# Logits, gate and row store of a chunk issued one loop step later in a gated linear attention + routed MoE kernel

## Chip, cores and metric

The kernel runs on one core of one Trainium2 chip. The metric is the device time of one execution in microseconds (us), the median of several runs. A core has five engines, each with its own instruction queue, worked off in order: TensorE (PE in the profile; its weight loads are PEld), VectorE (DVE), ScalarE (ACT), GpSimd (POOL) and SyncE (SP, which here only issues DMAs). The engines meet through semaphores: an instruction at the head of a queue that has to wait holds everything behind it on that engine.

## What is computed

A gated recurrence over 768 positions for 4 batches and 8 heads of width 48, whose output rows (3072 of 384 numbers) go through a mixture of 8 experts, each row through the expert with the highest logit:

```python
for t in range(S):
    state = alpha[:, :, t, :, None] * state + np.einsum('bhd,bhe->bhde', k[:, :, t], v[:, :, t])
    y[:, :, t] = np.einsum('bhd,bhde->bhe', q[:, :, t], state)
...
logits = x @ w_gate
expert_idx = np.argmax(logits, axis=1)
logits_s = logits - logits.max(-1, keepdims=True)
probs = np.exp(logits_s)
probs /= probs.sum(-1, keepdims=True) + 1e-09
gate_w = probs[np.arange(N), expert_idx]
...
    h = np.maximum(x_sorted[lo:hi] @ w1[e], 0.0)
    y_sorted[lo:hi] = h @ w2[e]
...
return (gate_w[:, None] * y).astype(np.float32)
```

Since the experts are piecewise linear without bias, a row can be scaled by its gate weight before it goes in.

## The kernel before

**Two halves.** The first (up to about 160 us) does the recurrence in 24 chunks of 128 positions (6 stretches of time for 4 batches; chunk s is batch s % 4 of stretch s // 4) and stores for each chunk 128 finished rows, scaled by their gate weight, to the scratch tensor x_rows. Then comes routing (lines 500 to 622) and the experts, which gather their rows from x_rows. Only the loop of the first half (lines 456 to 492) is touched by the change.

**The loop.** Its body is an order written out by hand under a manual schedule: each engine gets its instructions in the order of the calls, and step i mixes work on several chunks. `do(f, n)` calls f for chunk n if there is such a chunk. In step i, by engine:

- SP: `loads_for(i + 3)` starts the loads of a, v, k, q some chunks ahead, two chunks in each load, so a batch of four loads every other step; `keep_rows` issues the store of 128 rows (L411); `fetch_part` (L185, L188) one piece of the first expert's weights in steps 4 to 13; a small load at L264 once per four steps.
- PE: `scores(i)` (L311, into PSUM tiles sA and sB), at steps 4, 8, ... 20 `decay_cols` (L281, tile ep), `transposes(i + 1)` (L299, tile tp), `cums` (L250, tile cum, for chunk i + 5, the last in step 18), `read_state(i)` (L338), `attend(i)` (L348), `keys_values(i)` (L359), `rows(i - 1)` (L384: turned result back to rows, and the logits in the same product, into PSUM tile x).
- ACT: `result(i - 1)` (L367, copy of y to yT), `logs` (L244), the copy of the turned keys kT (L304), `cums`' two exponentials (L253, L254) and the issue of up to two tiny DMAs (L262: the one from icp for chunks 4 to 23, the one from cp for chunks 0 to 19), then `gate(i - 1)` (L402, an exponential and the reading of its accumulator) and `keep_rows(i - 1)` (L410, tile xs).
- DVE: `add_state(i - 1)` (L375/L377, tile acc), at a decay step the copy of E (L283), the two masked copies dA and dB (L319), the copy of the turned queries qT (L302), `decay_rows` (L269, L270) in the step ahead of a decay step, `logits(i - 1)` (L395, L396), two small operations of `gate` (L403, L404).
- POOL: `operands(i + 2)` (L289, two products), `scale_state(i)` (L326, tile U), and small things.

**What ties steps together.** Tiles sA, sB, x and cum have one buffer each (cum and ep share it), y is one tile for all steps. So `rows(i - 1)` may write x only after L395 and L410 have read the chunk before; `read_state(i)` may write y only after L367 and L377 have read chunk i - 1. yT and acc read different columns of y.

```python
            d["x"] = ps.tile([C, NP, C], F32, name="x")
...
            nc.vector.reduce_sum(lgn[:, t, :], d["x"][:, :, D2 : D2 + E].rearrange("p m e -> p e m"), axis=AX)
            nc.vector.tensor_reduce(lmin[:, t : t + 1], lgn[:, t, :], axis=AX, op=ALU.min)
...
            nc.scalar.activation(xs[:], d["x"][:, :, :D2], AF.Copy, scale=d["gw"][:])
            nc.sync.dma_start(x_d[t * C : (t + 1) * C, :], xs[:].rearrange("p m d -> p (m d)"))
```

Of the kernel before, what the change touches and what calls it, by code (L numbers as in the profile page):

```python
# [18 lines left out]
def kernel(  # L19
# [31 lines left out]
    NT = N // C  # L51
# [39 lines left out]
    def second_consts():  # L91
        nc.vector.tensor_scalar_mul(iw[:, :, D2:], iw[:, :, D2:], -1.0)
        for i in range(2):
            nc.vector.tensor_copy(
                iw[i * DP : (i + 1) * DP, :, i * D : (i + 1) * D],
                ident[i * DP : (i + 1) * DP, None, i * DP : i * DP + D].to_broadcast([DP, NP, D]),
            )
# [21 lines left out]
    def late_consts(i):  # L119
        if i == 0:  # L120
            nc.gpsimd.memset(lt_strict[:], 1.0)
            nc.gpsimd.affine_select(
                lt_strict[:], lt_strict[:], compare_op=ALU.is_gt, fill=0.0,
                base=0, pattern=[[1, C]], channel_multiplier=-1,
            )
            nc.gpsimd.memset(ones_sq[:], 1.0)
        if i == 1:
            nc.gpsimd.memset(zero_e[:], 0.0)
            nc.gpsimd.memset(keep[:], 1.0)
            nc.gpsimd.memset(keep[:, :, 0:1], 0.0)  # L130
        if i in (2, 3):
            for ti, tf, pattern, base, mult in list(iotas.values())[3 * (i - 2) : 3 * (i - 1)]:
                nc.gpsimd.iota(ti[:], pattern=pattern, base=base, channel_multiplier=mult)
                nc.gpsimd.tensor_copy(tf[:], ti[:])
            if i == 2:

                nc.gpsimd.memset(key0[:, 0:1], float(16 * N))
        if i == 4:

            nc.gpsimd.tensor_copy(iota_r[:], iota_f[:])  # L140
            nc.gpsimd.tensor_scalar(
                tok_n[:], tokv[:, NT // 2 :], scalar1=-1.0, scalar2=float(N // 2), op0=ALU.mult, op1=ALU.add,
            )
            nc.gpsimd.tensor_copy(tokv[:, NT // 2 :], tok_n[:])
# [33 lines left out]
    def fetch_part(g, i):  # L178

        if i == 0:  # L180
            g["w1"] = wpool.tile([C, DB, F], F32, name="w1")
            g["w2"] = wpool.tile([C, FB, Dm], F32, name="w2")
        if i < 6:
            a, h = i // 2, i % 2
            nc.sync.dma_start(g["w1"][:, a, h * F // 2 : (h + 1) * F // 2], moe_w1[0, a * C : (a + 1) * C, h * F // 2 : (h + 1) * F // 2])  # L185
        else:
            f = 2 * (i - 6)
            nc.sync.dma_start(  # L188
                g["w2"][:, f : f + 2], moe_w2[0, f * C : (f + 2) * C, :].rearrange("(a p) d -> p a d", p=C),
            )  # L190
# [27 lines left out]
    with tc.tile_pool(name="ld", bufs=6) as ld, \  # L218
# [23 lines left out]
        def logs(s):  # L242
            t = work.tile([C, Dm], F32, name="lna", bufs=4)
            nc.scalar.activation(t[:], st[s]["a"].rearrange("s h d -> s (h d)"), AF.Ln)  # L244
            st[s]["lna"] = t

        def cums(s):
            c, b = cb(s)
            cum = ps.tile([C, 512], F32, name="cum")
            nc.tensor.matmul(cum[:, :Dm], lhsT=cum_m[:], rhs=st[s]["lna"][:], start=True, stop=True)  # L250
            cp = work.tile([C, Dm], F32, name="cp", bufs=6)
            icp = work.tile([C, Dm], F32, name="icp", bufs=6)
            nc.scalar.activation(icp[:], cum[:, :Dm], AF.Exp, scale=-1.0)  # L253
            nc.scalar.activation(cp[:], cum[:, :Dm], AF.Exp)  # L254
            st[s]["cp"], st[s]["icp"] = cp, icp


            for cc, i, row in ((c, 1, icp[0:1, :]), (c + 1, 0, cp[C - 1 :, :])):
                if 0 < cc < NB:
                    if cc not in decay:  # L260
                        decay[cc] = work.tile([B, 2, Dm], F32, name="dec", bufs=3)
                    nc.scalar.dma_start(decay[cc][b : b + 1, i, :], row)  # L262
            if b == 0 and c + 1 < NB:
                nc.sync.dma_start(alpha0[:, c + 1], alpha[:, :, (c + 1) * C, :])  # L264

        def decay_rows(c):
            t = by_half(er[:B])
            d = decay[c].rearrange("b i (a p d) -> b i a p d", a=2, p=NP)
            nc.vector.tensor_tensor(t, d[:, 0], d[:, 1], op=ALU.mult)  # L269
            nc.vector.tensor_tensor(t, t, alpha0[:, c].rearrange("b (a p) d -> b a p d", a=2), op=ALU.mult)  # L270
# [7 lines left out]
        def decay_cols(c):  # L278
            ep = ps.tile([C, NP, C], F32, name="ep", tag="cum")
            for p in range(NP):  # L280
                nc.tensor.transpose(ep[:, p, :], pair(er[:], p), ident[:])  # L281
            decay[c] = work.tile([C, NP, B], F32, name="E", bufs=2)
            nc.vector.tensor_copy(decay[c][:], ep[:, :, :B])  # L283
# [130 lines left out]
        def do(f, i, *a):  # L414
            if 0 <= i < NT:
                f(i, *a)
# [4 lines left out]
        def sums_to(i):  # L421
            return {-2: 0, -1: 1, 0: 3, 1: 5}.get(i, -1 if i < 0 else min(i + 5, NT - 1))

        def new_sums(i):
            return range(sums_to(i - 1) + 1, sums_to(i) + 1)
# [10 lines left out]
        def loads_for(i):  # L436
            loads(("a", sums_to(i + 1)), ("v", i), ("k", i + 2), ("q", i + 2))

        def idle(n):

            t = ps.tile([C, NP, C], F32, name="sA")
            for _ in range(n):
                nc.tensor.matmul(t[:, :2, :], lhsT=er[:, 0].rearrange("s a d -> s (a d)"), rhs=er[:, :2], start=True, stop=True)
# [9 lines left out]
        nc.vector.memset(y[:], 0.0)  # L453
        first_consts()
        idle(4)
        for i in range(-4, NT + 1):
            loads_for(i + 3)
            do(scores, i)
            do(result, i - 1)
            do(add_state, i - 1)  # L460
            for s in new_sums(i + 1):
                logs(s)
            if 0 < i < NT and i % B == 0:
                decay_cols(i // B)
            do(mask, i, 0)
            do(mask, i, 1)
            if -2 < i < 0:
                idle(3)
            do(transposes, i + 1)
            sums = list(new_sums(i))  # L470
            for s in sums[:1]:
                cums(s)
            do(operands, i + 2)
            do(scale_state, i)
            if 0 < i + 1 < NT and (i + 1) % B == 0:
                decay_rows((i + 1) // B)
            do(read_state, i)
            do(attend, i)
            for s in sums[1:]:
                cums(s)  # L480
            do(keys_values, i)
            do(rows, i - 1)
            do(logits, i - 1)
            do(gate, i - 1)
            do(keep_rows, i - 1)
            if i == -3:
                second_consts()
            late_consts(i - 1)
            if 4 <= i < 14:
                fetch_part(groups[0], i - 4)  # L490
            if 15 <= i < 23:
                next(first_sums)
# [446 lines left out]
```

## Time and profile before

| what | value |
|---|---|
| median of 3 runs | 466.21 us (466.08 to 467.35) |
| the profiled execution, its own time | 467.84 us |
| its span | 466.0 us |
| granted TensorE clock, mean | 0.953 |
| busy: PE, DVE, ACT, POOL | 410.4, 229.8, 167.7, 140.2 us |
| copy of y to yT (L367), start for chunk 0, 3, 4, 14, 18, 19, 20, 23 | 17.72, 38.50, 45.01, 104.81, 128.87, 134.70, 140.87, 157.23 us |
| from one such start to the next, ordinary step | 5.82 to 5.84 us |
| the same, decay step 8, 12, 16 | 6.58 to 6.59 us |
| last logits (L395) | 159.56 us |

"Span" runs from the first to the last instruction that the profiler recorded; the execution's own time holds start and end besides. A line of the timeline gives start, duration, engine, line, operation, result and operands, and in brackets how long the engine had stood idle before it and what ended that. A PE line with x16 stands for sixteen matmuls one after the other. The start of the copy to yT comes once in each step, so its distances are the lengths of the steps.

### The profile page before, as it was taken

What the parts mean: (1) busy time and instruction counts of PE and PEld (TensorE: products, weight loads), DVE (VectorE), ACT (ScalarE), POOL (GpSimd) and SP (SyncE); (2) the same over time, 40 slices, a digit from 0 to 9 for tenths busy, and PEclk for the clock granted to TensorE, in tenths of its full rate; (3) what the DMA queues carried; (4) which work ended last, traced back from release to release, by engine and by line L of the source; (5) the groups of instructions that cost most, each with busy time, mean ns of one, the idle gap of its engine ahead of it and who ended that gap; (6) DMA issues with size and microseconds to landing.
All of it is one profiled execution on the core that took longest, in us unless ns stands there. A gap on an engine that the chain in (4) does not pass through costs nothing.

```text
span 466.0 us, 9245 instructions
## 1 busy us (share of the span) xinstructions
PE 410.4 (88%) x3548; PEld 350.4 (75%) x3548; DVE 229.8 (49%) x640; ACT 167.7 (36%) x454; POOL 140.2 (30%) x169
## 2 busy tenths in 40 slices
PE   7879999999987413799999999999999999999991
PEld 5657777777776401696996997997988988979970
DVE  3345454545455294357258258257356474473500
ACT  4564545454534200240351351440441522513511
POOL 3445444445663026500032032041140140200102
PEclk9999999999999555899999999999999999999997
DMA  9999999997621145303414415414423442400001
GB/s 178 213 181 214 216 201 216 211 240 167 137 70 35 40 146 193 109 0 136 152 41 188 153 38 188 153 48 175 153 88 133 169 170 64 152 1 18 30 1 49
DMA packets 119969, 59.07 MB, mean 127 GB/s; under 512 B 102806, under 2 KB 114159, under 8 KB 119924
## 3 DMA queue, kind: packets, MB, share of 16 engines
q1 hardware_dynamic: 114804, 48.80, 40.0%
q0 software_dynamic: 3424, 9.59, 5.9%
q8 instruction: 29, 0.48, 0.4%
q10 hardware_dynamic: 1696, 0.08, 0.2%
q14 instruction: 16, 0.13, 0.1%
HBM read 48.95 MB, written 9.58 MB: 126 GB/s over the span
## 4 chain that ended last, share of the span: by engine, by line
PE 57%; issue 7%; DVE 5%; ACT 3%; POOL 2%; DMA 1%; POOLq 0%; ACTq 0%; DVEq 0%
PE pA L729 12%; PE pB L729 9%; PE pA L785 8%; PE pC L800 8%; PE pC L729 5%; PE pB L785 4%; PE pC L785 2%; PE y L348 2%; PE x L384 2%; PE tp L647 2%; PE tp L830 1%; PE y L338 1%; ACT xs L410 1%; ACT yT L367 1%; PE sA L311 1%
## 5 line engine op out<-in xcount | busy, mean ns | idle before, releaser
L817 POOL DMA_INDIRECT out_dram<-zo,s_idx x29 | 31.8, 1096 | 210.0 <-ACT zo L816 114.3
L673 ACT COPY u<-pA 128x212 f32<-128x212 f32 (+7 forms) x80 | 25.5, 319 | 83.1 <-PE pA L785 77.6
L173 DVE TENSOR_TENSOR h_sb<-pB,u 128x212 f32<-128x212 f32 (+7 forms) x64 | 23.1, 362 | 64.0 <-PE pB L729 47.7
L800 PE MATMUL pC<-h_sb,w 128*128 128x424 f32 (+7 forms) x128 | 43.9, 496 | 0.0
L289 POOL TENSOR_TENSOR kqb<-k_sb,icp 128x384 f32<-128x384 f32 x24 | 25.5, 1062 | 60.6 <-PE y L359 23.2
L800 PEld LDWEIGHTS pC<-h_sb,w 128*128 128x128 f32 x128 | 24.1, 190 | 16.0 <-issue 6.7
L729 PE MATMUL pA<-t,s 128*128 128x212 f32 (+7 forms) x128 | 32.9, 339 | 2.4 <-issue 0.9
L637 POOL DMA_INDIRECT xg<-x_rows,g_idx x29 | 29.9, 1033 | 10.7 <-issue 6.4
L729 PE MATMUL pA<-xgT,w 128*128 128x212 f32 (+7 forms) x128 | 32.4, 335 | 0.0
L673 ACT COPY p<-pA 128x212 f32<-128x212 f32 (+7 forms) x40 | 13.1, 328 | 42.3 <-DVE t L176 26.9
L176 DVE TENSOR_TENSOR th<-h_sb,th 128x212 f32<-128x212 f32 (+7 forms) x64 | 23.2, 363 | 10.3 <-ACT h_sb L742 9.5
L311 PE MATMUL sA<-qT,kT 48*128 48x128 f32 x192 | 27.7, 284 | 0.2 <-DVE qT L302 0.2
L311 PE MATMUL sB<-qT,kT 48*128 48x128 f32 x192 | 27.7, 285 | 0.0
L402 ACT ACTIVATE gex<-lgn,lmin 128x8 f32<-128x8 f32 x24 | 7.2, 301 | 56.7 <-DVE lmin L396 54.5
L299 PE MATMUL tp<-ident,kqb 128*128 128x128 f32 x192 | 26.4, 279 | 1.2 <-POOL kqb L289 1.2
L729 PE MATMUL pC<-xgT,w 128*128 128x212 f32 (+7 forms) x128 | 27.4, 338 | 0.0
L729 PE MATMUL pB<-t,w 128*128 128x212 f32 (+7 forms) x128 | 27.0, 333 | 0.0
L311 PEld LDWEIGHTS sA<-qT,kT 48*128 48x128 f32 x192 | 23.1, 187 | 3.8 <-ACT kT L304 0.8
L384 PE MATMUL x<-iw,yT 128*64 128x104 f32 x384 | 23.0, 265 | 2.9 <-ACT yT L367 2.9
L742 ACT ACTIVATE h_sb<-h_sb 128x424 f32<-128x424 f32 (+7 forms) x32 | 17.1, 533 | 23.2 <-DVE h_sb L173 23.2
L785 PE MATMUL pA<-th,s 128*128 128x212 f32 (+7 forms) x128 | 24.6, 335 | 0.5 <-ACT u L673 0.5
L729 PEld LDWEIGHTS pA<-t,s 128*128 128x128 f32 x128 | 21.2, 190 | 4.9 <-ACT u L673 3.4
(176 smaller groups left out, 933.7 us busy)
## 6 DMA issues: line engine op xcount, KB each, us to landing
w<-in_moe_w_dram SPq DMA_DIRECT2D x14, 1536.0 KB, 7.4
x_rows<-xs SPq DMA_DIRECT2D x24, 192.0 KB, 2.1
a_sb<-in_alpha_dram SPq DMA_DIRECT2D x11, 384.0 KB, 4.3
k_sb<-in_k_dram SPq DMA_DIRECT2D x11, 384.0 KB, 5.7
q_sb<-in_q_dram SPq DMA_DIRECT2D x11, 384.0 KB, 5.3
v_sb<-in_v_dram SPq DMA_DIRECT2D x11, 384.0 KB, 5.6
w<-in_moe_w_dram SPq DMA_DIRECT2D x6, 256.0 KB, 3.7
w<-in_moe_w_dram SPq DMA_DIRECT2D x4, 384.0 KB, 3.8
```

The lines of the kernel that those rows point to most:

```text
L173: eng.tensor_tensor(out, a, b, op=ALU.add)
L176: eng.tensor_tensor(out, a, b, op=ALU.subtract)
L289: nc.gpsimd.tensor_tensor(by_half(kq[:, i]), d[n].rearrange("s (a p) d -> s a p d", a=2), d[e][:].rearrange("s (a p d) -> s a p d", a=2, p ...
L299: nc.tensor.transpose(tp[:, p, :], pair(kqb[s % 3][:, i], p), ident[:])
L311: nc.tensor.matmul(t[:, p, :], lhsT=d["kT"][r : r + D, p, :], rhs=d["qT"][r : r + D, p, :], start=True, stop=True,)
L384: nc.tensor.matmul(d["x"][o : o + HC, m, : D2 + E], lhsT=d["yT"][:, m // 2, m % 2, o : o + HC], rhs=iw[:, m, :], start=True, stop=True,)
L637: nc.gpsimd.indirect_dma_start(out=g["xg"][:r, j, :], out_offset=None, in_=x_d[:, :], in_offset=bass.IndirectOffsetOnAxis(ap=g["gi"](j, r) ...
L673: nc.scalar.copy(t[:, :m], bank["A"][:, :m])
L729: nc.tensor.matmul(out, lhsT=ops[n_][0], rhs=ops[n_][1], start=first and n_ == names[0], stop=True, skip_group_check=True,)
L785: nc.tensor.matmul(out, lhsT=lhs, rhs=rhs, start=first and f == 0, stop=True, skip_group_check=True)
L800: nc.tensor.matmul(d2[:, :n], lhsT=w2[:, f, 2 * C :], rhs=h[:, f, :n], start=(f == 0), stop=(f == FB - 1),)
L817: ins = nc.gpsimd.indirect_dma_start(out=out[:, :], out_offset=bass.IndirectOffsetOnAxis(ap=g["si"](j, r), axis=0), in_=zo[:r], in_offset= ...
```

## The change

In step i, `logits`, `gate` and `keep_rows` now work on chunk i - 2 in place of i - 1. `logits` stands behind the masks and ahead of `transposes`, `gate` and `keep_rows` stand behind `transposes` and ahead of `cums`. `rows` keeps its place at the end of the step. The loop has one step more, in which only these three have a chunk. Nothing is added or removed otherwise: the same instructions with the same shapes.

```diff
-        for i in range(-4, NT + 1):
+        for i in range(-4, NT + 2):
...
             do(mask, i, 1)
             if -2 < i < 0:
                 idle(3)
+            do(logits, i - 2)
             do(transposes, i + 1)
+            do(gate, i - 2)
+            do(keep_rows, i - 2)
             sums = list(new_sums(i))
...
             do(keys_values, i)
             do(rows, i - 1)
-            do(logits, i - 1)
-            do(gate, i - 1)
-            do(keep_rows, i - 1)
             if i == -3:
                 second_consts()
```

On each engine the order of a step becomes: DVE acc, (E), dA, dB, lgn, lmin, qT, the two of gate, (decay rows); ACT yT, lna, kT, gex, xs, icp, cp, the DMA issues of L262; SP the loads, then the store of chunk i - 2, then the small load and the weight piece; PE and POOL as before.

## Prediction
> **What bounds the kernel now.** I read the table by stages first. TensorE is near full in the chunk loop, and the clock is granted in full until the loop's end:
>
> ```profile
> 60.00:80.00 20.00, 19.10 (x307) 15.32 (x304) 9.57 (x30) 9.85 (x26) 9.28 (x11) 1.00 1.01 212
> 135.00:152.00 17.00, 13.21 (x225) 11.20 (x226) 9.00 (x25) 6.09 (x16) 7.54 (x9) 1.00 0.11 38
> 152.00:165.00 13.00, 5.64 (x67) 4.74 (x56) 4.57 (x22) 2.42 (x7) 0.00 (x0) 0.54 0.12 44
> ```
>
> The columns are PE, PEld, DVE, ACT, POOL, then the clock. 19.10 of 20 says that little can be won in the steady loop, but a modelled busy time can hide short waits. So I read the timeline of one ordinary step:
>
> ```profile
> 74.42 0.58 ACT L410 ACTIVATE xs<-x,gw 128x384 f32<-128x384 f32 x1 [0.47 <-PE sB L311]
> 74.90 0.58 ACT L367 COPY yT<-y 128x512 f32<-128x512 f32 x1
> 75.58 0.36 DVE L377 TENSOR_TENSOR acc<-y,U 128x192 f32<-128x192 f32 x1 [1.24 <-ACT yT L367]
> 75.85 0.68 DVE L319 TENSOR_TENSOR dA<-sA,cmask 128x512 f32<-128x512 f32 x1
> 76.08 0.66 PE L338 MATMUL y<-qT,U 48*48 48x128 f32 x16 [0.23 <-DVE acc L377]
> 76.25 0.51 ACT L253 ACTIVATE icp<-cum 128x384 f32<-128x384 f32 x1
> 76.80 0.51 ACTq L262 DMA_DIRECT2D dec<-icp  x1
> 77.40 0.54 ACTq L262 DMA_DIRECT2D dec<-cp  x1
> 78.02 0.90 PE L384 MATMUL x<-iw,yT 128*64 128x104 f32 x16
> 78.97 0.19 DVE L395 TENSOR_REDUCE lgn<-x 128x8 f32<-128x32 f32 x1 [1.24 <-PE x L384]
> 79.19 0.16 DVE L396 TENSOR_REDUCE lmin<-lgn 128x1 f32<-128x8 f32 x1
> 79.39 0.30 ACT L402 ACTIVATE gex<-lgn,lmin 128x8 f32<-128x8 f32 x1 [2.24 <-DVE lmin L396]
> 79.81 0.15 DVE L403 TENSOR_SCALAR gw<-gw 128x1 f32<-128x1 f32 x1 [0.46 <-ACT gex L402]
> 80.00 0.16 DVE L404 RECIPROCAL gw<-gw 128x1 f32<-128x1 f32 x1
> 80.26 0.58 ACT L410 ACTIVATE xs<-x,gw 128x384 f32<-128x384 f32 x1 [0.48 <-DVE gw L404]
> ```
>
> It is a ring. From x, lgn, lmin, gex and gw lead to xs; behind xs on ACT stands yT; acc waits for yT; read_state (L338) waits for acc, and leads through attend to the next rows (L384). ACT is idle 2.24 + 0.48 us in it, although y was ready for yT long before. Length 5.83 us.
>
> **The new order, step by step.** Let 0 be the start of scores.
>
> *PE without waits* (starts to starts, cum from 21.19 to 22.03, the last five from 40.45 to 43.13): scores 1.09, transposes 0.93, cum 0.84, read_state 0.58, attend 0.47 + 0.44, keys 0.36, rows 0.83: 5.54. A decay step has ep besides, 0.49: 6.03. So the most to win is 0.29 in an ordinary step and 6.59 − 6.03 = 0.56 in a decay step (0.48 in step 4).
>
> *A new ring, on ACT and DVE.* xs now stands behind kT and ahead of icp, cp and the two DMA issues; behind those stands the next step's yT. On DVE acc stands ahead of the masks, and the masks, lmin and qT ahead of gw. The hops: xs to icp 0.48 (as xs to yT); icp to the end of the second issue 1.69 (76.25 to 77.94); to yT 0.08; yT to acc 0.68; acc to dA 0.27; dA, dB 0.60 each; lgn to lmin 0.22; lmin to qT 0.08 (an operation that waits for nothing starts some 0.08 ahead of the end of the one before); qT 0.60; gw to reciprocal 0.19; to xs 0.26. Sum 5.75. gex hides beside qT: gw needs lmin + 0.62, qT gives lmin + 0.68. Does a DMA issue hold ACT back? Two rows say so:
>
> ```profile
> 17.12 0.50 ACTq L262 DMA_DIRECT2D dec<-cp  x1
> 17.72 0.59 ACT L367 COPY yT<-y 128x512 f32<-128x512 f32 x1 [0.63 <-ACT cp L254]
> ...
> 30.14 1.20 ACTq L262 DMA_DIRECT2D dec<-cp  x1
> 31.39 0.30 ACT L402 ACTIVATE gex<-lgn,lmin 128x8 f32<-128x8 f32 x1 [1.51 <-DVE lmin L396]
> ```
>
> yT and gex start 0.10 and 0.05 behind the issue; lmin had ended at 30.57. Today the issues lie in the 2.24 us in which ACT idles; that cover goes. The Trainium skill (DMA: Bandwidth & Descriptors, Issuing engines are not separate DMA queues) calls the sequencer time of an issue usually small beside its DMA; here 1.05 us per step stands on the path. Left at nothing, the rule makes the steady loop TensorE-bound (459.9 below).
>
> *Who waits behind it.* rows(i−1) is the added wait: x has one buffer, so it waits for xs(i−2). In the ring xs starts at 4.29, ends 4.87, rows can start at 4.92 where PE is there at 4.71: 0.21 idle per step, with the next scores queued behind. A decay step: ep ends at 1.75, E at 1.80, dA 1.88, xs 4.43, rows 5.06, before PE's 5.20: TensorE-bound at 6.03. POOL is covered: U ends 2.57 behind keys (78.20 to 80.77), read_state comes 3.69 behind. kT, qT end well ahead of the next scores.
>
> *SP.* The store waited for xs until 1.99 behind the next scores; now xs ends 0.9 ahead of them, so the loads behind it come 2.9 earlier. What covers them now: k and q of chunk 14 issue at 72.71 and 75.24, land after 5.7 and 5.3 (medians), and are used at 84.17 and 85.42, some 5 us later.
>
> *Steps 15 to 18* have one issue (1.05 in place of 1.69): ring 5.11, so PE's 5.54 and 6.03 hold. Step 15 still begins behind two: 5.75.
>
> *Steps without cum* (19 on): scores end at 1.16, dA 1.21, xs 3.76 (dA to xs 2.55), ends 4.34, rows 4.39, next scores 5.22, PE waiting for xs. Before: step 19 5.82, steps 21 and 22 5.06 and 5.05. Here the change loses 0.16 and 0.17, for gw now stands behind masks and qT. Step 20 (decay): rows 5.06, 5.89 against 6.02.
>
> *End.* Step 23 has no qT: xs 3.70, rows 4.33 against 4.44. rows(23) no longer waits for xs(22) and then yT(23), only for xs(22): 157.38 against 157.86.
>
> *Start.* Step 1 loses its gate: yT(1) can start at 23.87 in place of 25.21. But the second cum of step 2 waits for exponentials that now stand behind xs(0): about 28.75 against 28.00. With the later steps followed through, scores(4) start between 36.4 and 37.0, against 36.62. I take 0, bounds −0.4 and +0.3.
>
> **Sum of gains.** Ordinary steps 5 to 14: 8 × 0.08 = 0.64. Decay steps 4, 8, 12: 0.48 + 0.56 + 0.56 = 1.60. Steps 15 to 18: 0.08 + 0.55 + 0.29 + 0.29 = 1.21. Step 19: 0.60. Steps 20 to 22: 0.13 − 0.33 = −0.20. End: 0.11 + 0.48 = 0.59. Together 4.44. The profiled execution took 467.84 (span 466.0), 1.63 above the median of 466.21; routing and experts should not change, so 467.84 − 4.44 = 463.40, and against the median **461.8 us**.
>
> **The clock** could spoil the end. It was granted in full to about 152 and at 0.54 from then, behind a wait of PE of 1.58 us ahead of 151.70. In the new steps 21 and 22 PE waits about 0.9 once per step, where it waited 0.56. From no row can I read how much idling is allowed; if the clock fell one step earlier, step 22's 4.34 us of matmuls would double: bounds 0 and 4.3; I take 0, 0.9 being nearer to 0.56 than to 1.58. The Trainium skill (TensorE: Matmul & The Clock Gate, Part 1) has the clock halve after about 3.4 us of idleness in a window; by it the sum stays as it is.
>
> **Rivals.**
> 1. *The issues hold nothing* (both rows above being chance): xs to yT is 0.48 + 0.39 + 0.46 in place of 2.25, the ring 4.83, and PE bounds all steps to 18. Nine steps gain 0.21 more: 1.9, **459.9**. Against it: those two rows.
> 2. *The loads set the pace to step 14.* The DMA share is 1.01 in 60 to 80 us. Then 4 to 14 gain nothing (−2.24): **464.0**. Against it: SP stands idle 54.83 to 56.79 and 66.44 to 69.20, waiting for xs, and slack of 5 us.
> 3. *Slower: long DMA issues, now on the path.* The second issue took 1.20 at 30.14 and 1.67 at 41.73 (0.55 median), both hidden today. At 1.20 throughout, the ring is 6.40: the eight ordinary steps and step 15 lose 0.57 in place of gaining 0.08 (−5.85), decay steps take 6.48 in place of 6.03 (−1.35): **469.0**. From a mean of 0.63 an ordinary step is longer than before, from about 0.96 the whole kernel (9 × 0.41 + 3 × 0.23 is 4.4; a decay step's copy of E gives it 0.18 of slack). For it: loads now start nearer to these issues. Against it: 18 of 20 were short, beside running loads too.
> 4. *It moves the wait and wins nothing in the end*: PE waits for xs where it waited for acc, the waits of 0.9 are what the clock's governor counts, and the clock falls a step sooner: 461.8 + 4.3 = **466.1**. For it: the clock fell in this same stretch, behind waits of 0.56 and 1.58. Against it: 0.56 per step did not do it for steps 21 and 22.
>
> **Chances.** Forecast 0.52, rival 1 0.14, rival 2 0.12, rival 3 0.13, rival 4 0.09. The likeliest alone lies between 460.6 and 463.2 (ring ± 0.1 over eight steps, start ± 0.4). For eight in ten: down to 459.6, up to 465.6. About 0.3%, 1.4 us, can be told from no change. Faster 0.76 (the first three cases, nearly whole), same 0.11, slower 0.13.
>
> **What would show it.** yT starting 0.1 behind the second L262; acc, dA following at 0.68 and 0.95; rows waiting some 0.2 for xs in ordinary steps to 14 and 0.9 in 19, 21, 22; steps of 5.75, 6.03, then 5.54; L395's last near 155. I am wrong if ordinary steps stay at 5.83 or more, if read_state or the operands wait for a load, or if the clock falls before 147.

## The result, and the profile after

The changed kernel takes 461.22 us (median of 4 runs, 460.72 to 464.09) where the kernel before took 466.78 beside it (4 runs, 466.08 to 468.21): a ratio of 0.989, with a 95% interval of 0.984 to 0.994. The profiled execution took 461.57 us, its span is 459.7 (before: 467.84 and 466.0), at a mean granted clock of 0.956 (0.953).

The timeline of one ordinary step after the change, with ACT, DVE and, from PE, the product rows:

```profile
73.20 0.59 ACT L367 COPY yT<-y 128x512 f32<-128x512 f32 x1 [0.84 <-PE x L384]
...
73.89 0.36 DVE L377 TENSOR_TENSOR acc<-y,U 128x192 f32<-128x192 f32 x1 [2.90 <-ACT yT L367]
74.16 0.68 DVE L319 TENSOR_TENSOR dA<-sA,cmask 128x512 f32<-128x512 f32 x1
...
75.36 0.18 DVE L395 TENSOR_REDUCE lgn<-x 128x8 f32<-128x32 f32 x1
...
75.65 0.68 DVE L302 COPY qT<-tp 128x512 f32<-128x512 f32 x1
...
76.43 0.16 DVE L404 RECIPROCAL gw<-gw 128x1 f32<-128x1 f32 x1
76.62 0.58 ACT L410 ACTIVATE xs<-x,gw 128x384 f32<-128x384 f32 x1 [0.46 <-DVE gw L404]
...
77.26 0.93 PE L384 MATMUL x<-iw,yT 128*64 128x104 f32 x16
77.61 0.50 ACTq L262 DMA_DIRECT2D dec<-icp  x1
78.21 0.55 ACTq L262 DMA_DIRECT2D dec<-cp  x1
78.80 0.58 ACT L367 COPY yT<-y 128x512 f32<-128x512 f32 x1 [0.84 <-PE x L384]
```

The rows give 5.60 us from yT to yT, and every hop can be read as a distance of starts. yT begins at 78.80, where the second issue ends at 78.76; the release that the bracket names, rows, is not what came last. DVE works from acc to the reciprocal without a gap, then ACT from xs through icp, cp and the two issues to yT: the two halves of the new ring. The old one is gone: gex no longer stands on ACT waiting for the logits of rows that PE has only just finished.

The lengths of the steps, from the start of scores in one step to the next, tell where the time went (both profiled executions):

| steps | before | after |
|---|---|---|
| start of scores(4) | 36.62 | 36.73 |
| 4, 8, 12, 16 (decay) | 6.51, 6.58, 6.57, 6.58 | 5.88, 5.88, 6.39, 5.89 |
| 5, 6, 7 | 5.82, 5.83, 5.83 | 5.65, 5.60, **6.58** |
| 9, 10, 11 | 5.83, 5.83, 5.84 | **6.20**, 5.60, 5.60 |
| 13, 14, 15 | 5.84, 5.83, 5.83 | 5.68, 5.61, 5.60 |
| 17, 18 | 5.83, 5.83 | 5.44, 5.45 |
| 19, 20 | 5.82, 6.02 | 5.16, 5.84 |
| 21, 22 | 5.06, 5.05 | 5.22, 5.23 |
| start of scores(23) | 148.95 | 145.23 |

Three steps are out of line: 7, 9 and 12. ACT's timeline tells of 7 and 12:

```profile
58.94 0.58 ACT L410 ACTIVATE xs<-x,gw 128x384 f32<-128x384 f32 x1 [1.44 <-DMA x_rows<-xs]
...
83.82 1.24 ACTq L262 DMA_DIRECT2D dec<-cp  x1
85.10 0.59 ACT L367 COPY yT<-y 128x512 f32<-128x512 f32 x1 [1.54 <-issue]
```

In step 7, xs waits for a store of x_rows to land, because tile xs has two buffers and the store of two chunks ago still reads one. In step 12 a single issue takes 1.24 us and yT stands behind it; so it is in step 9, with one of 1.19 at 66.37.

The stages of the changed kernel in the windows (PE, PEld, DVE, ACT, POOL, clock, DMA share, GB/s):

```profile
60.00:80.00 20.00, 19.45 (x309) 16.05 (x306) 8.83 (x28) 11.26 (x28) 8.93 (x11) 1.00 1.04 223
...
148.00:152.70 4.70, 1.35 (x24) 0.89 (x20) 1.00 (x7) 2.42 (x7) 0.00 (x0) 1.00 0.12 44
152.70:165.00 12.30, 2.65 (x20) 2.26 (x20) 8.84 (x42) 0.97 (x3) 0.00 (x0) 0.50 0.12 35
```

PE is still not full between 60 and 80 us, 19.45 of 20. At the end the clock is whole until 152.70, and half from there. Before, it was already halved when rows(22) began. The last two products rows (of chunks 22 and 23) of the changed kernel, from PE's timeline:

```profile
149.69 0.93 PE L384 MATMUL x<-iw,yT 128*64 128x104 f32 x16 [1.27 <-ACT xs L410]
152.73 1.65 PE L384 MATMUL x<-iw,yT 128*64 128x104 f32 x16 [2.11 <-ACT xs L410]
```

Only rows(23) is slow here (1.65), where before rows(22) at 153.39 took 1.61 and rows(23) 1.65. The last logits (L395) start at 154.43 in place of 159.56.

### The profile page after: what moved, and what is told of

Read it like the earlier page. It is cut to its first block, busy times and chain, and to the rows that moved or that the text cites. A ratio compares the mean times of both kernels' runs of the same rounds, so it can differ in the third digit from the quotient of the medians.

```text
span 459.7 us, 9241 instructions
## 1 busy us (share of the span) xinstructions
PE 410.2 (89%) x3548; PEld 351.1 (76%) x3548; DVE 228.4 (50%) x640; ACT 171.1 (37%) x454; POOL 140.5 (31%) x169
## 4 chain that ended last, share of the span: by engine, by line
PE 64%; DVE 10%; issue 8%; DMA 6%; ACT 5%; POOL 2%; SPq 2%; ACTq 1%; POOLq 0%; DVEq 0%
PE pA L729 12%; PE pB L729 9%; PE pA L785 8%; PE pC L800 8%; PE pC L729 5%; PE pB L785 4%; PE x L384 3%; PE sA L311 3%; PE pC L785 2%; DMA w<-in_moe_w_dram 2%; DVE dA L319 2%; DVE dB L319 2%; DVE qT L302 2%; PE tp L647 2%; PE y L348 2%
## 5 line engine op out<-in xcount | busy, mean ns | idle before, releaser
L729 PE MATMUL pA<-t,s 128*128 128x212 f32 (+7 forms) x128 | 33.2, 341 | 1.0 <-ACT u L673 0.4
L729 PE MATMUL pA<-xgT,w 128*128 128x212 f32 (+7 forms) x128 | 32.4, 335 | 0.0
L729 PE MATMUL pC<-xgT,w 128*128 128x212 f32 (+7 forms) x128 | 27.4, 338 | 0.0
L729 PE MATMUL pB<-t,w 128*128 128x212 f32 (+7 forms) x128 | 27.0, 333 | 0.0
L384 PEld LDWEIGHTS x<-iw,yT 128*64 128x64 f32 x384 | 18.2, 140 | 9.9 <-ACT xs L410 9.4
L289 POOL TENSOR_TENSOR kqb<-q_sb,cp 128x384 f32<-128x384 f32 x24 | 24.7, 1029 | 2.1 <-DMA q_sb<-in_q_dram 2.1
L377 DVE TENSOR_TENSOR acc<-y,U 128x192 f32<-128x192 f32 x16 | 5.7, 358 | 39.0 <-ACT yT L367 26.7
```

What stands on the lines that cost most here:

```text
L289: nc.gpsimd.tensor_tensor(by_half(kq[:, i]), d[n].rearrange("s (a p) d -> s a p d", a=2), d[e][:].rearrange("s (a p d) -> s a p d", a=2, p ...
L384: nc.tensor.matmul(d["x"][o : o + HC, m, : D2 + E], lhsT=d["yT"][:, m // 2, m % 2, o : o + HC], rhs=iw[:, m, :], start=True, stop=True,)
L729: nc.tensor.matmul(out, lhsT=ops[n_][0], rhs=ops[n_][1], start=first and n_ == names[0], stop=True, skip_group_check=True,)
```

## Experiments

The theory: in the changed kernel a ring over ACT and DVE sets an ordinary step, and the two DMA issues of L262 are a part of it; before, they lay in ACT's idle time. The rivals: the issues hold nothing; TensorE or the loads set the step; the moved logits and gate gain by themselves. Where a line number in these profiles is larger by one or two, the edit has added lines above.

### The issues doubled, after and before

Each DMA of L262 is issued a second time from ACT, into a scratch tensor that nothing reads.

```diff
+        spare = nc.dram_tensor("spare", (NT, 2, Dm), F32, kind="Internal").ap()
...
                     nc.scalar.dma_start(decay[cc][b : b + 1, i, :], row)
+                    nc.scalar.dma_start(spare[s : s + 1, i, :], row)
```

In the changed kernel:

> The changed kernel, with each of the small DMAs of L262 issued a second time from ACT, into a scratch tensor that nobody reads. Ring theory (an issue holds ACT, and it now stands between xs and the next yT): each step up to 14 gets about 1.15 us longer (two more issues of 0.55 to 0.60), ordinary steps 5.60 -> 6.75, steps 15 to 18 about 5.6; whole kernel 471 to 475 us. Rival (issues hold nothing, TensorE is the bound): steps stay at 5.60, whole kernel 461 us, within 1.

Measured 474.70 us (2 runs), 1.016 of the kernel before (1.012 to 1.020), and 13.5 above the changed kernel. Its timeline on ACT:

```profile
79.39 0.44 ACTq L264 DMA_DIRECT2D spare<-icp  x1
...
80.49 0.45 ACTq L264 DMA_DIRECT2D spare<-cp  x1
80.98 0.59 ACT L369 COPY yT<-y 128x512 f32<-128x512 f32 x1 [1.78 <-PE sB L313]
```

Two more issues of 0.44 and 0.45 make an ordinary step 6.55 in place of 5.60, and yT again stands right behind the last of them. Steps 17 and 18 issue one DMA of L262, now two; they stay at 5.45 and 5.44. There xs to yT takes 2.02, which makes the ring 5.44, no longer than PE's own work in a step. So where the ring is the longest path, the issues are on it at their full price.

In the kernel before:

> The kernel before with the same doubling. Ring theory: ACT idles 2.24 us behind these issues until lmin comes, so 1.15 us more are hidden: ordinary steps stay at 5.83, whole kernel 466 to 468 us (the first steps with two prefix sums may lose 1 us). Rival (an issue costs the same wherever it stands): 11 steps of +1.15, 478 us or more.

Measured 470.01 us (8 runs), ratio 1.006 (1.004 to 1.009). Two places of ACT's timeline:

```profile
25.25 0.30 ACT L404 ACTIVATE gex<-lgn,lmin 128x8 f32<-128x8 f32 x1 [1.77 <-DMA spare<-icp]
...
80.80 0.45 ACTq L264 DMA_DIRECT2D spare<-cp  x1
81.74 0.30 ACT L404 ACTIVATE gex<-lgn,lmin 128x8 f32<-128x8 f32 x1 [2.24 <-DVE lmin L398]
```

In the steady loop the last of four issues ends at 81.25, and gex begins 0.5 later, when lmin is ready: hidden, and most ordinary steps stay at 5.83. The loss is larger than expected and comes for the most part from the start (scores(4) at 38.57 in place of 36.62), where steps 1 and 2 each have two cumulated sums and so eight issues. Step 2 takes 9.67 in place of 6.81. The gex at 25.25 (before: 23.86) stands behind issues that end at 25.21, though lmin had ended at 23.55; so xs comes 1.61 later in the step. For the rest of the step's loss, the granted clock fell: 0.69 between 28 and 33 us, where it was 1.00, and rows took 1.62 in place of 0.90.

### The issues on SP instead of ACT, after and before

```diff
-                    nc.scalar.dma_start(decay[cc][b : b + 1, i, :], row)
+                    nc.sync.dma_start(decay[cc][b : b + 1, i, :], row)
```

In the changed kernel:

> The changed kernel with the small DMAs of L262 issued from SP in place of ACT. Ring theory: xs to yT falls from 2.18 to about 1.35, the ring to 4.8, TensorE bounds the ordinary steps at about 5.44 (as in step 17 today), and the two long issues (1.19 and 1.24 us) cost nothing any more: 8 x 0.16 + 1.3 = 2.6 us less than the changed kernel, 458 to 459 us. Rival (ring broken but the loads behind the new waits on SP come late): operands wait for k or q, 461 us or more.

Measured 481.01 us (4 runs), ratio 1.029 (1.026 to 1.033): a miss. Steps 5, 6 and 9 do come at 5.44 or 5.45, so with the issues gone from ACT the ring is gone too. But SP works its queue off in order, and the small transfers now stand behind the bulk loads. Once issued they land after 1.9 and 2.2 us (medians; from ACT in the changed kernel 3.8 and 3.5), so it is their turn in the queue that comes late. The waits of this kernel (total, times, longest), from 41 to 130 us:

```profile
DVE er L269 <- DMA dec<-icp: 26.2, 4, 7.9
```

Step 4 takes 14.73. Neither the theory's 458 to 459 us nor the rival's late k and q foresaw this. The edit is not clean: it removes one cost and adds another.

In the kernel before:

> The kernel before with the small DMAs issued from SP. Ring theory: they lay in 2.24 us of idle ACT time, so nothing changes: ordinary steps 5.83, 466 to 467 us. Rival (ACT was short of time in the kernel before as well): faster by 2 us or more.

Measured 483.33 us (4 runs), ratio 1.035 (1.030 to 1.040), with the same lateness (step 4: 16.71). Here the undisturbed ordinary steps are 5.97 and 5.98, against 5.83: taking the issues away from ACT shortened nothing, as ACT wasn't short of time. That they are 0.14 longer was not expected; gex now starts 0.26 behind lmin (0.20 before) and xs 0.34 behind the reciprocal (0.26), and why, no run shows.

### Only the row store moved

The logits and the gate are put back to chunk i − 1 at the end of the step; only keep_rows stays behind the turned keys, with chunk i − 2.

```diff
-            do(logits, i - 2)
             do(transposes, i + 1)
-            do(gate, i - 2)
             do(keep_rows, i - 2)
...
             do(rows, i - 1)
+            do(logits, i - 1)
+            do(gate, i - 1)
```

> Only the third of the three moved calls: logits and gate stay on chunk i-1 at the end of the step, keep_rows goes to chunk i-2 behind the copy of kT. Theory: what made the old ring long was xs ahead of yT, waiting for gw; with xs alone moved yT starts behind gex, about 0.9 earlier, that ring falls to about 4.9, and the new ring over the masks doesn't arise, since gw no longer stands behind masks and qT. So TensorE bounds: ordinary steps about 5.44, steps 21 and 22 about 4.4 instead of 5.22; whole kernel 455 to 458 us, faster than the changed kernel. Rival (the wait for lmin at gex still holds yT, ACT's time is the bound): ordinary steps 5.6 to 5.8, 461 to 464 us.

Measured 454.85 us (6 runs), ratio 0.977 (0.974 to 0.981): better than the changed kernel. One step on ACT, and the window that was not full:

```profile
75.96 0.30 ACT L402 ACTIVATE gex<-lgn,lmin 128x8 f32<-128x8 f32 x1 [2.18 <-DVE lmin L396]
...
76.26 0.56 ACT L367 COPY yT<-y 128x512 f32<-128x512 f32 x1
...
77.20 0.58 ACT L304 COPY kT<-tp 128x512 f32<-128x512 f32 x1
77.78 0.58 ACT L410 ACTIVATE xs<-x,gw 128x384 f32<-128x384 f32 x1
```

```profile
60.00:80.00 20.00, 20.00 (x332) 16.32 (x331) 11.79 (x33) 12.29 (x30) 7.82 (x10) 1.00 1.05 237
```

gex still waits its 2.18 us, and again covers the issues (the last ends at 74.58). But the gate factor is made in that place, ahead of yT and kT, so xs starts as soon as kT is done, and yT no longer stands behind it. PE is full: undisturbed ordinary steps are 5.44 or 5.45 (step 5 takes 6.53, behind a wait of xs for a store), decay steps 5.88 or 5.89, and steps 19, 21 and 22 take 4.80, 4.42 and 4.43 where the changed kernel takes 5.16, 5.22 and 5.23. So moving xs is what breaks the old ring; moving logits and gate with it, to where the change puts them, builds the new one.

### Logits ahead of the masks, gate ahead of the transposes

```diff
+            do(logits, i - 2)
             do(mask, i, 0)
             do(mask, i, 1)
...
-            do(logits, i - 2)
-            do(transposes, i + 1)
             do(gate, i - 2)
+            do(transposes, i + 1)
             do(keep_rows, i - 2)
```

> The changed kernel with logits one place earlier (ahead of the masks) and gate ahead of transposes, so that on DVE the two small operations of gate stand ahead of qT. Theory: acc to xs falls from 2.73 to about 2.14, the ring from 5.60 to 5.0, TensorE bounds ordinary steps at 5.44; in steps 19 to 22 xs no longer keeps rows waiting (5.22 -> about 4.4): 4 to 6 us less, 455 to 457 us. Rival (late steps are bound by something else, POOL's U or the masks): only 8 x 0.16 is won, 459.5 to 460.5 us.

Measured 457.18 us (6 runs), ratio 0.981 (0.978 to 0.984). With all three still on chunk i − 2, but the logits no longer behind the masks and gw no longer behind qT, the undisturbed ordinary steps are 5.44 to 5.47, and steps 21 and 22 are 4.42 and 4.43: it was the order on DVE that made the new ring too long. What keeps it above the expected 455 to 457 is in part a wait for the store in step 11 (7.28), on ACT's timeline:

```profile
81.47 0.58 ACT L410 ACTIVATE xs<-x,gw 128x384 f32<-128x384 f32 x1 [3.32 <-DMA x_rows<-xs]
```

### A third buffer for xs

To make room, icp goes from 6 buffers to 5.

```diff
-            icp = work.tile([C, Dm], F32, name="icp", bufs=6)
+            icp = work.tile([C, Dm], F32, name="icp", bufs=5)
...
-            xs = work.tile([C, NP, D2], F32, name="xs")
+            xs = work.tile([C, NP, D2], F32, name="xs", bufs=3)
```

With the changed kernel:

> The changed kernel with three buffers for xs instead of two (and five instead of six for icp, to make room). In the changed kernel's profile xs of step 7 waited 1.0 us more than usual, for the landing of a store, and the step took 6.58 in place of 5.60. Theory (the buffer comes back late, since the store stands behind four loads on SP): no such wait, 460 to 460.7 us. Rival (chance of that one execution): no change, 461.2 us.

Measured 460.70 us (4 runs), ratio 0.988 (0.985 to 0.991). Step 7 is 5.60, and no xs waits for a store from step 4 on. That doesn't prove the cause of the long step 7, since the unedited kernel, run once more, has a step 7 of 5.61 too (below); the cause is read from the timeline of step 7 itself. The runs (459.88 to 461.70) overlap those of the changed kernel, so a gain of the whole isn't shown either.

With only the row store moved:

> keep_rows alone moved, with three buffers for xs (and five for icp). In the profile with keep_rows alone, four waits of xs for the landing of a store are left, 4.2 us together, one of which made step 6 6.53 us long in place of 5.44. Theory: they go, 453 to 454.5 us. Rival (those waits lie in ACT time that nobody needs, but for one of that execution): as keep_rows alone, 455 us.

Measured 453.62 us (5 runs), ratio 0.970 (0.967 to 0.974). This is the fastest version of all, ahead of both kernels, though its runs (451.69 to 454.05) overlap those with two buffers (453.85 to 459.22). The ordinary steps are 5.44 or 5.45, and what is late next is seen in its waits (total, times, longest) from 41 to 125 us:

```profile
POOL kqb L289 <- DMA k_sb<-in_k_dram: 7.0, 2, 3.8
```

Step 16 takes 6.97 and step 14 6.07; loads of k now reach POOL late.

### Doubled issues where only the row store moved

The edit of the first experiment, put on top of the kernel with only keep_rows moved.

> keep_rows alone moved, with the small DMAs of L262 issued twice as before. Theory: here ACT stands idle 2.18 us behind these issues again, waiting for lmin, so that 0.95 us more are hidden: ordinary steps stay at 5.44 and the kernel takes at most 4 us more (the start lost 1.3 to 2.9 us in the other two), 455 to 459 us. Rival (any kernel near TensorE's bound pays for them): 13 us more, 468 us.

Measured 459.30 us (2 runs), ratio 0.983 (0.979 to 0.988), 4.45 above the same kernel without doubling, where the changed kernel had lost 13.5. Six of its ordinary steps to 15 stay at 5.44 or 5.45: hidden again, under gex's wait. Of the loss, 2.37 lies ahead of scores(4), in the steps with eight issues; the rest is for the most part in single long steps (15 and 16: 7.61 and 7.50). The rival's price for every step doesn't come.

### The changed kernel once more

The same kernel, unedited, to see which of its odd steps come again.

> The changed kernel once more, beside the two above on one chip: 460.5 to 462 us; ordinary steps 5.60 again, and if the long issues (1.19 and 1.24 us) and the wait for a store in step 7 belong to the order of the program, they stand in the same steps; if they are chance, elsewhere or not at all.

Measured 461.24 us (6 runs, 460.24 to 461.98 and one of 467.42), ratio 0.986 (0.983 to 0.990). Undisturbed ordinary steps are 5.56 to 5.61 and decay steps 5.88 or 5.89 again. But now step 6 is the long one (6.41, an issue of 1.35 at 48.43), step 9 is 5.86 and step 11 5.98, while steps 7 and 12 are 5.61 and 5.89. So the long steps 6, 7 and 12 do not belong to the order of the program. For step 9 that stays open: in both executions, and in the one with three buffers (5.72), the second issue just ahead of its yT is long (1.19, 0.84 and 0.71).

## Why the prediction was right, step by step

The forecast was 461.8 and the time 461.22. Its mechanism held; several sizes were off. That the time came so near is in part luck. The gain forecast was 4.4 us, and the medians differ by 5.56; but the kernel before also took 0.57 more (466.78) than the median from which the forecast was subtracted. And of the 6.3 won between the profiled executions, 0.66 at the end and 1.13 behind the last logits stood in no term.

| term | gain forecast | gain measured |
|---|---|---|
| start, to scores(4) | 0 | −0.11 |
| steps 4 to 14 | 2.24 | 1.64 |
| steps 15 to 18 | 1.21 | 1.69 |
| step 19 | 0.60 | 0.66 |
| step 20, then 21 and 22 | 0.13, −0.33 | 0.18, −0.34 |
| end, scores(23) to the last logits | 0.59 | 1.41 |
| after the last logits | 0 | 1.13 |
| sum, profiled executions | 4.44 | 6.3 |

*The new ring* was right hop by hop, at 5.60 and not 5.75. xs to yT is 2.18 (forecast 2.25), yT to acc 0.69, acc to dA 0.27, then as forecast to qT, gw to the reciprocal 0.18, and from there to xs 0.19 where 0.26 was taken. The doubled issues (+0.95 a step after, hidden before) and the logits and gate moved ahead (5.44) show that it is this ring. The wait of rows for xs makes an ordinary step 0.16 longer than PE's own work (0.21 was forecast), and steps 21 and 22 0.80 (about 0.9).

*PE without waits* is 5.44, not 5.54 (steps 17 and 18, and the kernel with only the row store moved). Transposes, then cum take 1.67 together; the two starts read at 21.19 and 22.03 and the row of transposes gave 0.93 + 0.84 = 1.77. A decay step is 5.88, not 6.03. That makes steps 15 to 18 gain more than forecast.

*Steps 4 to 14* gained less all the same. At 5.60 and 5.88 throughout they would have won 8 × 0.23 + 0.63 + 0.70 + 0.69 = 3.86. Given back were 0.98 in step 7, 0.60 in step 9, 0.51 in step 12 and 0.13 in steps 5 and 13. Steps 9 and 12 are rival 3, the long issues, in two of eleven steps. Its point of decision, a mean of 0.63 for the second issue, was even passed: the eleven of steps 4 to 14 have a mean of 0.69. It was worked out from a ring of 5.75; from 5.60 the point is 0.55 + 0.23 = 0.78.

*Step 7* is what the paragraph on SP missed. It followed the loads that stand behind the store, and not the store that stands behind the loads. The xs of step 7 waits for the store of two chunks ago, whose own xs had been done at 47.35. SP's timeline in the changed kernel:

```profile
46.33 3.76 SPq L236 DMA_DIRECT2D v_sb<-in_v_dram  x1
...
51.77 1.44 SPq L236 DMA_DIRECT2D q_sb<-in_q_dram  x1
53.30 1.80 SPq L411 DMA_DIRECT2D x_rows<-xs  x1
```

The store is issued 5.9 us after its xs, and only at 58.94 can the xs of step 7 start. Before, the store behind the same loads went out at 52.91 for an xs done at 50.93. From issue to landing a store now takes 4.0 (median), where it took 2.1. With two buffers that sometimes is too late.

*The late steps* came as worked out, the losses of 21 and 22 too. The kernels with only xs moved and with the logits ahead of the masks, whose steps 21 and 22 are 4.42 or 4.43, show that this loss was the price of where gw stood on DVE, not of the store.

*The end* won 1.41, not 0.59. The term for rows(23) was right: from xs(22) to rows(23) takes 0.63 where it took 1.11. The 0.11 for rows(22) did not come: it starts 4.46 behind scores(23), where it started 4.44. Unforeseen was that the clock stayed whole for rows(22): from its start to lgn takes 0.98 where it took 1.64. Rival 4 looked for the opposite, a fall of the clock one step sooner. No term held this 0.66. Another 0.29 came from lgn to xs(22).

*After the last logits* nothing was forecast. From the last L395 to the first of the experts' products at L729 another 0.26 is won, and 0.87 from there to the first at L785; ahead of that one the trace shows PE waiting 0.95 and 0.85 before, and 0.42 after. No experiment tried this, so its cause stays open. The medians differ by 5.56 and the profiled executions by 6.27: the one of before lay 1.06 above the median of 466.78, the one of after 0.35 above 461.22.

*Rival 1* fell with the doubled issues. The sentence cited with it, that an issue's time is usually small beside its DMA (the Trainium skill, DMA: Bandwidth & Descriptors, Issuing engines are not separate DMA queues), holds here: an issue takes some 0.50 to 0.55, and from issue to landing the same DMAs take 3.5 to 3.8 (medians). But small beside its DMA is not free for the engine that issues: two more issues of 0.44 and 0.45 in a step cost 0.95. *Rival 2* fell with ordinary steps of 5.60 beside the same loads, and of 5.44 with only the row store moved; in the fastest version late loads do show.

## What to carry to other kernels

When a step is held because one instruction stands ahead of another on a queue, move that one instruction, and leave its preparation where the engine is idle anyway: the whole group moved won about 5.6 us, its last member alone about 11.7. A DMA issue on a compute engine is free only as long as that engine idles behind it, so before such idle time is used up, add the issues to the new chain. After a step is made shorter, look for the buffer that comes free only when a DMA lands, and for what that DMA stands behind.

## What the runs showed of the hardware

Forty tiny DMAs, moved from ACT's queue to that of SP, came so late behind bulk loads that four waits for them took 26.2 us, and the whole took 20 us more (16 in the kernel before). The issue of a tiny DMA holds ACT for 0.44 to 0.66 us as a rule, but 0.7 to 1.7 now and then, and mostly in other steps in another execution. The clock's fall at the end doesn't follow the longest single wait of PE: it was halved behind a wait of 2.11 in the changed kernel (rows(23) took 1.65), and still whole behind 2.23 with the logits ahead of the masks (0.93). In both the kernel before and the changed one it fell behind single waits (1.58 and 2.11) well short of the idleness in the rule that the prediction cites. What does decide it stays open.
